# A window-attention and gated-MLP kernel on one core: the q/k/v products of two chunks as 2x2 block products, k and v parked in DRAM, attention in the background

## The chip, the core and the metric

The kernel runs on one core of a Trainium2 chip. The core has TensorE (PE in the profile; PEld are its weight loads), VectorE (DVE), ScalarE (ACT), GpSimd (POOL) and SyncE (SP), which here only issues DMA transfers. The metric is the time of one execution on the device, in microseconds (us); lower is better.

## The reference

```python
xn = layernorm(x)                      # x: 2048 x 1024, bf16
q, k, v = split(xn @ wqkv)             # 32 heads of 32
# a token at s sees the 8 tokens s, s-2, ..., s-14
attn = softmax(q . k[s - 2w] * 32**-0.5, over w = 0..7; masked below 0)
s = (sum_w attn[w] * v[s - 2w]) @ wo
h = silu(xn @ w1) * (xn @ w3)          # 1024 -> 3584
g = silu(h @ w2)                       # 3584 -> 1024
out = x + s * g
```

## The kernel before

The 2048 tokens are four chunks of 512 (`c` 0 to 3). Two chunks are a pair (`b` 0 and 1), and the MLP works on a pair. Activations lie transposed: a feature is a partition, tokens are columns. A matmul here is 128x128 by 128x512 into a bank of PSUM; there are eight banks (pool `mm`).

**Block products.** The up and down products of a pair are computed with seven block products in place of eight (Winograd's form of Strassen): rows are the two chunks, columns two halves of the output features, and the inner dimension is cut into two halves. The sums of blocks of the activations are made once a pair (`xn_sums`: `xs0` to `xs3`; `s1` to `s4` in `mlp_down`). The sums of blocks of the weights are made for pair 0 (`w_sums`, `w2_sums`), stored in DRAM (`s_dram`, `t_dram`) and read again for pair 1. In such a group ScalarE copies a bank into another (`fork`) or to SBUF (`us5`, `us2`), and VectorE adds from PSUM (`ua2`, `uh`; `dsa`, `dsb` in the down product). One up step (`up_step`) makes 256 of the 3584 features with 56 matmuls; a pair has 14. Its `tail` is put into the instruction stream of the next step (`flush`). The q, k and v products are plain: `qkv_t(c, t, ...)`, 64 matmuls for a chunk and each of q, k, v, evicted by ScalarE.

**Attention** (`attention(c)`) is VectorE work: for each of the eight positions a product of q with the shifted kT (`qk`), then a tree of sums (`qa`, `qb`, `qc`) into E; 16 DMAs on GpSimd regroup E into L (a<-E in the profile); sums `z` and the softmax; 16 DMAs write it back (E<-a); and products with the shifted vT (`pv`, `pa`), which leave the result in the place of q (`qo`). kT and vT hold one chunk and 16 tokens ahead of it, which `halo` copies on GpSimd. `wo(c)` multiplies by wo, by the gate g, and adds x.

**Order.** Every operation is recorded with its cells (`plan.op`). TensorE's order is the order of the program. The order of the other engines' instructions comes from the planner (`Plan.simulate`): it goes through all operations with fixed costs, and an engine that is free takes, of what is ready, the operation with the earliest due time (`limits`: when TensorE needs its result). On the chip each engine then works strictly in the order written, SyncE's queue of transfers included. The chunks went

```python
qkv_t(c0, ...) ; xn_sums() ; up steps 0..cut ; attention(c0)
qkv_t(c1, ...) ; up steps cut..14            ; attention(c1)
mlp_down(b)    ; wo(c0)                      # wo(c1) after the next pair's q/k/v
```

Lines in the profile are those of helpers: L299 `mm`, L308 `tt` (VectorE's additions and products), L313 `cp`, L316 `silu`, L322 `dma`, L421 the transposes of x and L428 their copies (`ln_tp`), L396, L399, L402 and L409 the layernorm on ScalarE, L448 `halo`. Tiles: `r` weights, `k` 128x512 buffers (pool `k2`), `a` attention's buffers, `xs` the sums of xn and later the gates.

Of the kernel before, what the change touches and what calls it, by code (L numbers as in the profile page):

```python
# [193 lines left out]
def kernel(  # L194
# [44 lines left out]
    t_dram = dram.tile([P, FH, 4, CH], FP16, name="t_dram")  # L239

# [8 lines left out]
    E = const.tile([P, W, CH], BF16, name="E")  # L249
# [87 lines left out]

    def gt_cell(u, i):
        return ("xs", 2 * u + i // 4, i % 4)
# [106 lines left out]
    def halo(c):  # L446
        for nm, b in (("k", kT), ("v", vT)):
            plan.op(POOL, f"halo{nm}", lambda b=b: nc.gpsimd.tensor_copy(  # L448
                out=b[:, :, 0:HALO], in_=b[:, :, CH:CH + HALO]),
                [(nm, j) for j in range(NJ)], [(nm, j, "halo") for j in range(NJ)], 0.95)  # L450

    def qkv_t(c, t, wts):
        half = c % 2
        for j in range(NJ):
            if j == 2:
                flush()
            ps = bank(f"qkv{c}_{t}_{j}")
            for hf in range(2):
                mm(ps, [qkv_w(wts[hf], k, j) for k in range(4)],
                   [lambda k=k, hf=hf: xT[:, half, hf * 4 + k, :] for k in range(4)], hf == 0,  # L460
                   [wts[hf]] + xt_cells(half, hf), last=hf == 1)
            if t == 0:
                dst, wr = (lambda j=j: qo[:, half, j, :]), qo_cells(half, [j])
            elif t == 1:
                dst, wr = (lambda j=j: kT[:, j, HALO:HALO + CH]), [("k", j)]
            else:
                dst, wr = (lambda j=j: vT[:, j, HALO:HALO + CH]), [("v", j)]
            cp(f"ev{c}_{t}_{j}", dst, ps.ap, [ps], wr)


    def attention(c):
        u = c % 2
        J4 = [range(0, 4), range(4, 8)]
        r4 = lambda s: s.ap().rearrange("p (j n) -> p j n", j=4)
        for w in range(W):
            o = HALO - DIL * w
            pr = []
            for jh in range(2):
                p_t = plan.slot("att", f"p{c}_{w}_{jh}")
                tt(f"qk{c}", mul, lambda p_t=p_t: r4(p_t), lambda jh=jh: qo[:, u, jh * 4:jh * 4 + 4, :],  # L480
                   lambda jh=jh, o=o: kT[:, jh * 4:jh * 4 + 4, o:o + CH],
                   qo_cells(u, J4[jh]) + [("k", j) for j in J4[jh]] + ([("k", j, "halo") for j in J4[jh]] if w else []),
                   [p_t], 2048, True)
                pr.append(p_t)
            p0, p1 = pr
            tt(f"qa{c}", add, lambda p0=p0: r4(p0), lambda p0=p0: r4(p0), lambda p1=p1: r4(p1), [p0, p1], [p0], 2048, True)
            tt(f"qb{c}", add, lambda p0=p0: r4(p0)[:, 0:2], lambda p0=p0: r4(p0)[:, 0:2], lambda p0=p0: r4(p0)[:, 2:4],
               [p0], [p0], 1024, True)
            tt(f"qc{c}", add, lambda w=w: E[:, w, :], lambda p0=p0: r4(p0)[:, 0], lambda p0=p0: r4(p0)[:, 1],
               [p0], [("E", w, sq, r) for sq in range(4) for r in range(NR)], 512, True)  # L490
        L = [plan.slot("att", f"L{c}_{i}") for i in range(2)]
        Lv = lambda i: L[i].ap().rearrange("p (r w n) -> p r w n", r=2, w=W)
        for r in range(NR):
            for sq in range(4):
                dma(POOL, f"L{c}", lambda r=r, sq=sq: Lv(r // 2)[sq * 32:(sq + 1) * 32, r % 2, :, :],
                    lambda r=r, sq=sq: E[r:P:NR, :, sq * P:(sq + 1) * P],
                    [("E", w, sq, r) for w in range(W)], [(L[r // 2], r % 2, sq)], 128)
# [27 lines left out]
        for r in range(NR):  # L525
            for sq in range(4):
                dma(POOL, f"E{c}", lambda r=r, sq=sq: E[r:P:NR, :, sq * P:(sq + 1) * P],
                    lambda sq=sq: pbv()[sq * 32:(sq + 1) * 32], [pb], [("E", w, sq, r) for w in range(W)], 128)
        for jh in range(2):
            js = slice(jh * 4, jh * 4 + 4)  # L530
            A = lambda js=js: qo[:, u, js, :]
            Ac = qo_cells(u, J4[jh])

            def pv(dst, wr, w, jh=jh, js=js):
                o = HALO - DIL * w
                tt(f"pv{c}", mul, dst, lambda: E[:, w, :].unsqueeze(1).to_broadcast([P, 4, CH]),
                   lambda: vT[:, js, o:o + CH],
                   [("E", w, sq, r) for sq in range(4) for r in range(NR)] + [("v", j) for j in J4[jh]]
                   + ([("v", j, "halo") for j in J4[jh]] if w else []), wr, 2048, True)

            pv(A, Ac, 0)
            B = plan.slot("att", f"B{c}")
            pv(lambda B=B: r4(B), [B], 1)
            tt(f"pa{c}", add, A, A, lambda B=B: r4(B), Ac + [B], Ac, 2048, True)
            for w0 in (2, 4, 6):
                B, C = plan.slot("att", f"B{c}"), plan.slot("att", f"C{c}")
                pv(lambda B=B: r4(B), [B], w0)
                pv(lambda C=C: r4(C), [C], w0 + 1)
                tt(f"pa{c}", add, lambda B=B: r4(B), lambda B=B: r4(B), lambda C=C: r4(C), [B, C], [B], 2048, True)
                tt(f"pa{c}", add, A, A, lambda B=B: r4(B), Ac + [B], Ac, 2048, True)  # L550
# [47 lines left out]
    def up_step(b, fb):  # L598
# [5 lines left out]
        if fb + 1 < FB and (b, fb + 1) not in tiles and fb + 1 != cut[b]:  # L604
            up_load(b, fb + 1)
# [31 lines left out]
        if b == 0 and fb + 1 < FB and fb + 1 != cut[b]:  # L637
            w_sums(fb + 1)
        for i in I:
            mm(pb[i], sl(2, i), tx[2], False, [(st, 2)] + xs_cells(2))  # L640
            tt("uh", add, hv(i, 1), pb[i].ap, lambda i=i: f32(sp5[i]), [pb[i], sp5[i]], hc(i, 1), 512, False)
            sg2.append(plan.slot("k2", "sg2"))
            silu("sg2", lambda i=i: b16(sg2[i])[:, 0:CH], lambda i=i: f32(su2[i]), [su2[i]], [sg2[i]], 0.54)
# [5 lines left out]
        def tail():  # L649
            for i in I:  # L650
                mm(pb[i], wl(1, 1, i), tx[3], False, [(wt, 1, 1)] + xs_cells(3))
                tt("um", mul, hv(i, 0), hv(i, 0), pb[i].ap, hc(i, 0) + [pb[i]], hc(i, 0), 512, False)
            for i in I:
                tt("um2", mul, hv(i, 1), hv(i, 1), lambda i=i: b16(sg2[i])[:, 0:CH], hc(i, 1) + [sg2[i]], hc(i, 1), 512, True)
# [24 lines left out]
    gts = [xsb[:, 2 * u:2 * u + 2].rearrange("p a k n -> p (a k) n") for u in range(2)]  # L679

    def mlp_down(b):
# [29 lines left out]
        gt = gts  # L711
# [27 lines left out]
        for g in G:  # L739
            prod(pa[g], g, 0, 1, rhs, False, BF16)  # L740
            silu("dg", lambda g=g: gt[0][:, g], pa[g].ap, [pa[g]], [gt_cell(0, g)], 0.48)
# [18 lines left out]
        for g in G:  # L760
            prod(pe[g], g, 0, 1, rhs, False, FP16)
            tt("dsb", add, lambda g=g: f32(su2[g]), pe[g].ap, lambda g=g: f32(su2[g]), [pe[g], su2[g]], [su2[g]], 512, False)
            silu("dg", lambda g=g: gt[0][:, NST + g], lambda g=g: f32(su2[g]), [su2[g]], [gt_cell(0, NST + g)], 0.54)
        rhs = rhs_load("t", t=T3)
        for g in G:
# [4 lines left out]
            silu("dg", lambda g=g: gt[1][:, NST + g], lambda g=g: f32(sp5[g]), [sp5[g]], [gt_cell(1, NST + g)], 0.54)  # L770
        for st in range(NST if b + 1 < NB else 0):
            ln_tp(2 * b + 3, st, xn[1])
        rhs = rhs_load("t", t=T4)
        for g in G:
            prod(pb[g], g, 1, 1, rhs, False, BF16)
            silu("dg", lambda g=g: gt[1][:, g], pb[g].ap, [pb[g]], [gt_cell(1, g)], 0.48)

    def wo(c):
        u = c % 2
        gt = gts[u]  # L780
# [17 lines left out]
        for i, (dh, st) in enumerate(grp):  # L798
            if i + 2 < len(grp):
# [6 lines left out]
            o_t = plan.slot("k2", "o_t")  # L806
            tt("o_t", mul, lambda o_t=o_t: f32(o_t), ps.ap, lambda dh=dh, st=st: gt[:, dh * NST + st],
               [ps, gt_cell(u, dh * NST + st)], [o_t], 512, False)
            x = xe[i]
            tt("x_o", add, lambda x=x: b16(x)[:, CH:D], lambda o_t=o_t: f32(o_t), lambda x=x: b16(x)[:, 0:CH],  # L810
               [o_t, (x, 0)], [(x, 1)], 512, False)
# [4 lines left out]
    cut = (11, 10)  # L816
    x0 = plan.slot("r8", "x0")
# [8 lines left out]
    for b in range(NB):  # L826
        c0, c1 = 2 * b, 2 * b + 1
        if b:
            halo(c0)
        qkv_t(c0, 0, qkv_load(0))  # L830
        if b == 0:
            x1 = plan.slot("r8", "x1")
# [4 lines left out]
        wk = qkv_load(1)  # L837
        if b == 0:
            for st in range(NST):
                ln_tp(1, st, x1)  # L840
        qkv_t(c0, 1, wk)
        qkv_t(c0, 2, qkv_load(2))
        if b == 0:
            w2_load(0)
        else:
            wo(c0 - 1)
        xn_sums()
        for fb in range(cut[b]):
            up_step(b, fb)
        attention(c0)  # L850
        halo(c1)
        wq = qkv_load(0)
        wk = qkv_load(1)
        qkv_t(c1, 0, wq)
        wv = qkv_load(2)
        qkv_t(c1, 1, wk)
        up_load(b, cut[b])
        if b == 0:
            w_sums(cut[b])
        qkv_t(c1, 2, wv)  # L860
        for fb in range(cut[b], FB):
            up_step(b, fb)
        attention(c1)
        mlp_down(b)
        wo(c0)
    wo(2 * NB - 1)
# [31 lines left out]
```

## Time and profile before

| | us |
|---|---|
| median of 3 runs (lowest, highest) | 761.17 (760.47, 761.50) |
| profiled execution | 759.42 |
| its span, first to last instruction | 757.6 |
| TensorE busy | 742.4 |
| VectorE busy | 599.4 |
| ScalarE busy | 320.1 |
| GpSimd busy | 106.8 |

DMA moved 150.56 MB, 199 GB/s on the mean. The mean granted clock of TensorE was 0.995 of full speed. Rows give the mean time of one instruction and the idle time of the engine ahead of it with what ended it; a stretch of the table of windows has, for each engine, its busy time and the number of its instructions.

### The profile page before, as it was taken

The numbers are of one execution on the slowest core, as the hardware profiler recorded it, in microseconds if no ns is written. First come the engines' busy times: TensorE is split into PE (matmuls) and PEld (weight loads), VectorE is DVE, ScalarE is ACT, GpSimd is POOL, SyncE is SP. The second block draws the span as 40 slices with busy tenths as digits, with TensorE's granted clock in tenths as the row PEclk, the third lists the DMA queues.
The fourth block names the chain that finished last, engine by engine and source line by source line (L and its number), as shares of the span: only waits on it lengthen the run. The fifth ranks groups of instructions, "written<-read, shape, count | busy, mean of one in ns | idle before, by whom it ended". The sixth has DMA issues, their size and how long they took to land.

```text
span 757.6 us, 9366 instructions
## 1 busy us (share of the span) xinstructions
PE 742.4 (98%) x3457; PEld 375.8 (50%) x3516; DVE 599.4 (79%) x830; ACT 320.1 (42%) x535; POOL 106.8 (14%) x172
## 2 busy tenths in 40 slices
PE   7999999999999999998999999999999999999997
PEld 4664444444664444453566444444466544444443
DVE  6599988899989995539937995789925987939946
ACT  5536446544335599334033144644423544311200
POOL 0000050600311006140000004400100012040000
PEclk9999999999999999999999999999999999999999
DMA  9766589776598875766762847654554457483723
GB/s 326 228 223 200 162 194 306 241 259 199 185 304 263 286 239 147 211 183 227 250 196 98 260 148 192 195 174 149 167 163 143 140 166 188 147 235 126 224 87 120
DMA packets 123117, 150.56 MB, mean 199 GB/s; under 512 B 6080, under 2 KB 97728, under 8 KB 119488
## 3 DMA queue, kind: packets, MB, share of 16 engines
q1 hardware_dynamic: 114944, 119.55, 50.3%
q0 software_dynamic: 8128, 30.42, 12.7%
q8 instruction: 27, 0.44, 0.3%
q14 instruction: 18, 0.15, 0.1%
HBM read 115.34 MB, written 26.21 MB: 187 GB/s over the span
## 4 chain that ended last, share of the span: by engine, by line
PE 84%; DVE 5%; ACT 4%; DMA 3%; issue 2%; POOL 2%; SPq 0%; DVEq 0%; ACTq 0%
PE mm L299 83%; DVE a L308 3%; DMA a<-E 2%; POOL E L322 1%; ACT k L396 1%; ACT k L399 1%; DMA E<-a 1%; DVE k L308 1%; DVE r L308 1%; DVE h_sb L308 1%; PE mm L421 1%; POOL a L322 1%; DVE small L379 0%; ACT xT L428 0%; DMA r<-in_A_x_dram 0%
## 5 line engine op out<-in xcount | busy, mean ns | idle before, releaser
L299 PEld LDWEIGHTS <-r 128*128 128x128 bf16 (+1 forms) x2336 | 263.4, 113 | 241.1 <-issue 0.7
L299 PE MATMUL mm<-xT,r 128*128 128x512 bf16 x1395 | 322.9, 379 | 2.8 <-ACT xT L428 0.5
L299 PE MATMUL mm<-xs,r 128*128 128x512 f16 x896 | 207.7, 379 | 0.0
L299 PE MATMUL mm<-r,h_sb 128*128 128x512 f16 (+1 forms) x664 | 147.8, 382 | 0.4
L308 DVE TENSOR_TENSOR a<-qo,kT 128x2048 bf16<-128x2048 bf16 x64 | 76.6, 1217 | 39.7 <-ACT kT L313 39.6
L299 PEld LDWEIGHTS <-h_sb 128*128 128x128 bf16 (+1 forms) x672 | 65.9, 98 | 79.4 <-issue 2.4
L308 DVE TENSOR_TENSOR a<-a,a 128x2048 bf16<-128x2048 bf16 (+1 forms) x72 | 87.6, 1217 | 19.4 <-DMA a<-E 19.0
L313 ACT COPY k<-mm 128x512 f32<-128x512 f32 x128 | 74.4, 586 | 55.8 <-PE mm L299 55.3
L308 DVE TENSOR_TENSOR a<-E,vT 128x2048 bf16<-128x2048 bf16 x56 | 66.0, 1215 | 0.0
L308 DVE TENSOR_TENSOR k<-mm,k 128x512 f32<-128x512 f32 x72 | 48.0, 683 | 20.0 <-PE mm L299 18.0
L316 ACT ACTIVATE k<-k 128x512 bf16<-128x512 f32 x56 | 35.0, 630 | 51.5 <-DVE k L308 51.4
L313 ACT COPY mm<-mm 128x512 f32<-128x512 f32 x64 | 36.1, 570 | 47.2 <-PE mm L299 47.0
L299 PE MATMUL mm<-r,qo 128*128 128x512 bf16 x250 | 55.4, 379 | 0.3
L316 ACT ACTIVATE h_sb<-mm 128x512 bf16<-128x512 f32 x56 | 33.4, 597 | 52.2 <-PE mm L299 52.2
L322 POOL DMA_DIRECT2D a<-E x64 | 36.9, 585 | 90.1 <-DVE E L308 80.6
L322 POOL DMA_DIRECT2D E<-a x64 | 36.7, 581 | 73.3 <-DVE a L308 69.2
L308 DVE TENSOR_TENSOR a<-a 128x1024 bf16<-128x1024 bf16 (+4 forms) x60 | 37.7, 631 | 8.6 <-DMA a<-E 7.0
L308 DVE TENSOR_TENSOR h_sb<-h_sb,mm 128x512 bf16<-128x512 bf16 x56 | 36.9, 680 | 7.6 <-PE mm L299 7.5
L313 ACT CAST qo<-mm 128x512 bf16<-128x512 f32 x32 | 18.8, 586 | 54.1 <-PE mm L299 52.9
L308 DVE TENSOR_TENSOR r<-r 128x512 f16<-128x512 bf16 (+1 forms) x84 | 39.1, 503 | 2.9 <-PE mm L299 2.9
L299 PEld LDWEIGHTS <-qo 128*128 128x128 bf16 x256 | 25.1, 98 | 30.1
L308 DVE TENSOR_TENSOR qo<-qo,a 128x2048 bf16<-128x2048 bf16 x32 | 38.9, 1214 | 0.1
(61 smaller groups left out, 435.4 us busy)
## 6 DMA issues: line engine op xcount, KB each, us to landing
r<-in_B_w_dram SPq DMA_DIRECT2D x56, 512.0 KB, 5.4
r<-in_A_wqkv_dram SPq DMA_DIRECT2D x24, 1024.0 KB, 5.4
s_dram<-r POOLq DMA_DIRECT2D x14, 1024.0 KB, 6.1
r<-t_dram SPq DMA_DIRECT2D x16, 896.0 KB, 5.8
r<-s_dram SPq DMA_DIRECT2D x14, 1024.0 KB, 5.3
r<-in_B_w_dram SPq DMA_DIRECT2D x12, 896.0 KB, 5.9
r<-in_A_wo_dram SPq DMA_DIRECT2D x8, 1024.0 KB, 7.8
t_dram<-r POOLq DMA_DIRECT2D x14, 512.0 KB, 5.7
```

The lines of the kernel that those rows point to most:

```text
L299: nc.tensor.matmul(ps.ap(), lhsT=lhs[k](), rhs=rhs[k](), start=(first and k == 0), stop=(last and k == n - 1), skip_group_check=not (first ...
L308: plan.op(DVE, name, lambda: fn(out=o(), in0=a(), in1=b()), rd, wr, occ, 0.08, late=late)
L313: plan.op(ACT, name, lambda: nc.scalar.copy(out=o(), in_=a()), rd, wr, occ, 0.11)
L316: plan.op(ACT, name, lambda: nc.scalar.activation(out=o(), in_=a(), func=ACTF.Silu), rd, wr, occ, 0.11, table="silu")
L322: plan.op(eng, name, lambda: e.dma_start(out=o(), in_=a()), rd, wr, occ, 0.0, nbytes=kb * 1024, late=late)
L396: plan.op(ACT, f"mean{c}_{st}", lambda i=i, st=st, junk=junk: nc.scalar.activation(out=b16(junk), in_=xrow(xt, st), func=ACTF.Copy, scale= ...
L399: plan.op(ACT, f"var{c}_{st}", lambda i=i, st=st, junk=junk: nc.scalar.activation(out=b16(junk), in_=xrow(xt, st), func=ACTF.Square, bias= ...
L421: nc.tensor.matmul(tp.ap()[:, k * P:(k + 1) * P], lhsT=xrow(xt, st)[:, kt * P:(kt + 1) * P], rhs=ident[:], start=(k == 0), stop=(k == KH - ...
```

## The change

- q of chunks 0 and 1 stays plain (`q_plain`), with the transposes of chunk 1 in the middle of chunk 0's q. All other q/k/v products are made for a pair at once (`qkv_pairs`), with seven block products of eight; `qkv_sums` makes the weights' block sums on VectorE each time.
- kT and vT still hold one chunk. What comes early (k and v of chunks 1 and 2; q, k and v of chunk 3) is written into parts of `h_sb` that are not yet in use, stored to DRAM from there (`put`) and fetched by `attention` (`get`). `halo` is split into k's and v's.
- Attention is recorded elsewhere: chunk 0 after all up steps, chunk 1 inside pair 1 after up step 6, followed by `wo(1)`; chunk 2 after pair 1's up steps, chunk 3 after `wo(2)`.
- E is stored as four runs of 128 tokens with the eight positions in each, so a piece of 32 partitions is one run of 2 KB; half of the pieces' DMAs are issued by SyncE.
- In the up step's tail and in `wo`, ScalarE copies the product out as bf16, and VectorE works on bf16 in SBUF alone; the two products of the tail become one of 1024 columns.
- Gates lie in other places (`gate`), and chunk 3's transposes are taken one group at a time in the last group of the down product.

```diff
-    def qkv_t(c, t, wts):
+    def q_plain(c, wts, mid=None):
...
+    def put(c, nm):
...
+        dma(SP, f"put{nm}{c}", lambda: park[nm, c][:], src, cells, [("park", nm, c)], 1024)
+    def get(c, nm):
...
+        dma(SP, f"get{nm}{c}", dst, lambda: park[nm, c][:], [("park", nm, c)], wr, 1024)
+    def qkv_sums(wts):
+        S = [plan.slot("r8", f"S{i}") for i in range(2)]
+        w = lambda kh, r: (lambda: wts[kh].ap().rearrange("p (c j) -> p c j", j=NJ)[:, :, r * 4:r * 4 + 4])
...
+        tt("qs0", add, sv(0), w(0, 1), w(1, 1), wts, c(0), 2048, True)
+        tt("qs1", sub, sv(1), sv(0), w(0, 0), c(0) + [wts[0]], c(1), 2048, True)
+        tt("qs3", sub, sv(3), w(1, 0), sv(1), c(1) + [wts[1]], c(3), 2048, True)
+        tt("qs2", sub, sv(2), w(0, 0), w(0, 1), [wts[0]], c(2), 2048, True)
+    def qkv_pairs(b, nm, wts, S, load=None):
...
+                mm(pa[i], wl(0, js[i]), bx[0, 0], True, [wts[0]] + xt_cells(0, 0))
+                mm(pe[i], sw(0, js[i]), tx[0], True, sc(0) + xs_cells(0))
+                cp("qfork", pb[i].ap, pa[i].ap, [pa[i]], [pb[i]])
+                cp("qs5", lambda i=i, s=sp5: f32(s[i]), pe[i].ap, [pe[i]], [sp5[i]])
+                mm(pa[i], wl(1, js[i]), bx[0, 1], False, [wts[1]] + xt_cells(0, 1))
+                cp("qc11", dst, pa[i].ap, [pa[i]], wr)
+                mm(pb[i], sw(1, js[i]), tx[1], False, sc(1) + xs_cells(1))
+                cp("qu2", lambda i=i, s=su2: f32(s[i]), pb[i].ap, [pb[i]], [su2[i]])
+                mm(pe[i], sw(3, js[i]), bx[1, 1], False, sc(3) + xt_cells(1, 1))
+                tt("qc12", add, dst, pe[i].ap, lambda i=i, s=su2: f32(s[i]), [pe[i], su2[i]], wr, 512, False)
+                mm(pb[i], sw(2, js[i]), tx[2], False, sc(2) + xs_cells(2))
+                tt("qc22", add, dst, pb[i].ap, lambda i=i, s=sp5: f32(s[i]), [pb[i], sp5[i]], wr, 512, False)
+                    mm(pb[i], wl(1, js[i] + 4), tx[3], False, [wts[1]] + xs_cells(3))
+                    cp("qc21", dst, pb[i].ap, [pb[i]], wr)
...
     def attention(c):
+        for nm in "qk":
+            if nm == "k" and c:
+                halo("k")
+            if (nm, c) in park:
+                get(c, nm)
...
-                dma(POOL, f"L{c}", lambda r=r, sq=sq: Lv(r // 2)[sq * 32:(sq + 1) * 32, r % 2, :, :],
-                    lambda r=r, sq=sq: E[r:P:NR, :, sq * P:(sq + 1) * P],
+                dma((POOL, SP)[sq % 2], f"L{c}", lambda r=r, sq=sq: Lv(r // 2)[sq * 32:(sq + 1) * 32, r % 2],
+                    lambda r=r, sq=sq: E[r:P:NR, sq], [("E", w, sq, r) for w in range(W)], [(L[r // 2], r % 2, sq)], 96)
...
-                tt(f"pv{c}", mul, dst, lambda: E[:, w, :].unsqueeze(1).to_broadcast([P, 4, CH]),
-                   lambda: vT[:, js, o:o + CH],
+                q4 = lambda a: a.rearrange("p j (q n) -> p j q n", n=P)
+                tt(f"pv{c}", mul, lambda: q4(dst()), lambda: E[:, :, w, :].unsqueeze(1).to_broadcast([P, 4, NST, P]),
+                   lambda: q4(vT[:, js, o:o + CH]),
...
     (tail of the up step)
-                tt("um", mul, hv(i, 0), hv(i, 0), pb[i].ap, hc(i, 0) + [pb[i]], hc(i, 0), 512, False)
+                cp("uc", lambda i=i: b16(sg2[i])[:, 0:CH], pb[i].ap, [pb[i]], [(sg2[i], 0)])
-                tt("um2", mul, hv(i, 1), hv(i, 1), lambda i=i: b16(sg2[i])[:, 0:CH], ..., 512, True)
+                tt("um", mul, lambda i=i: h_sb[:, fl[i], :], lambda i=i: h_sb[:, fl[i], :], lambda i=i: b16(sg2[i]), ..., BL, True)
...
     (wo)
-            tt("o_t", mul, lambda o_t=o_t: f32(o_t), ps.ap, lambda dh=dh, st=st: gt[:, dh * NST + st], ..., 512, False)
-            tt("x_o", add, lambda x=x: b16(x)[:, CH:D], lambda o_t=o_t: f32(o_t), lambda x=x: b16(x)[:, 0:CH], ..., 512, False)
+            cp("s_c", xv, ps.ap, [ps], [(x, 1)])
+            tt("s_g", mul, xv, xv, gv, [(x, 1)] + gc, [(x, 1)], CH, True)
+            tt("x_o", add, xv, xv, lambda x=x: b16(x)[:, 0:CH], [(x, 0), (x, 1)], [(x, 1)], CH, True)
...
     (mlp_down, last group)
-        for st in range(NST if b + 1 < NB else 0):
-            ln_tp(2 * b + 3, st, xn[1])
         rhs = rhs_load("t", t=T4)
         for g in G:
+            if b + 1 < NB:
+                ln_tp(2 * b + 3, g, xn[1])
             prod(pb[g], g, 1, 1, rhs, False, BF16)
...
     (the order)
+        qkv_pairs(b, "v", wv, sv, first)
+        for fb in range(FB):
             up_step(b, fb)
+            if b and fb == 6:
+                attention(c0 - 1)
+                wo(c0 - 1)
         attention(c0)
         mlp_down(b)
         wo(c0)
-    wo(2 * NB - 1)
+    attention(3)
+    wo(3)
```

## The prediction

> **What bounds the kernel now.** I read the busy times of the page first, then the waits of TensorE, the chain of waits that ended last, and a table of stretches around the one place where that chain leaves TensorE.
>
> ```profile
> PE 742.4 (98%) x3457; PEld 375.8 (50%) x3516; DVE 599.4 (79%) x830; ACT 320.1 (42%) x535; POOL 106.8 (14%) x172
> PE   7999999999999999998999999999999999999997
> PE mm L421 <- ACT xT L428: 3.1, 1, 3.1
> PE mm L421 <- DVE r L385: 2.6, 1, 2.6
> PE mm L299 <- ACT xT L428: 0.5, 1, 0.5
> ```
>
> TensorE is busy 98% of the span, and past the head (12.9 us) it has one long wait: 3.1 us for the transposes of x (L421). So a matmul taken away is worth its full time, provided that nobody else becomes late. The chain and the stretches show what that one wait cost:
>
> ```profile
> 269.03 0.48 ACT mm L313
> ...
> 329.96 5.63 DMA E<-a
> 343.97 0.61 DVE k L308
> 344.60 0.63 ACT xs L316
> 345.23 1.95 ACT xT L428 x4
> 347.60 13.99 PE mm L299 x57
> ```
>
> ```profile
> 341.00:347.60 6.60, 3.05 (x35) 2.16 (x34) 6.60 (x8) 4.19 (x10) 0.00 (x0) 1.00 1.00 317
> 347.60:350.00 2.40, 2.40 (x7) 0.88 (x6) 2.40 (x3) 2.05 (x5) 0.00 (x0) 0.50 1.01 372
> 350.00:352.00 2.00, 2.00 (x9) 0.75 (x7) 2.00 (x3) 0.00 (x0) 0.00 (x0) 0.75 1.04 372
> ```
>
> Attention of chunk 1 wrote its softmax back late (E<-a); VectorE, in order, held the additions of the down product (k, `dsa`) behind the products that needed E; ScalarE held the copies of the transposes (xT) behind the gates (xs) of those additions; TensorE stood still for 6.60 - 3.05 = 3.55 us, and then ran at a granted clock of 0.50 for 2.4 us and 0.75 for 2.0 us, which loses 1.2 + 0.5 = 1.7 us. The place costs 5.2 us.
>
> VectorE's price per instruction is the step from one start to the next, since ends overlap by about 0.08 us:
>
> ```profile
> 246.07 0.42 DVE L308 TENSOR_TENSOR E<-a 128x512 bf16<-128x512 bf16 x1
> 246.41 0.68 DVE L308 TENSOR_TENSOR h_sb<-h_sb,mm 128x512 bf16<-128x512 bf16 x1
> 247.01 2.35 DVE L308 TENSOR_TENSOR a<-qo,kT 128x2048 bf16<-128x2048 bf16 x2
> 249.28 0.42 DVE L308 TENSOR_TENSOR r<-r 128x512 f16<-128x512 bf16 x1
> ```
>
> 512 columns of 16 bits in SBUF: 0.34 us; 512 with an operand in PSUM: 0.60; 2048 of 16 bits: 2.27 / 2 = 1.135; by the same reading 1024 of 16 bits 0.60 (starts 256.26 and 256.86). A ScalarE eviction steps by 0.48 (first line of the chain above).
>
> **Part 1, the products.** Before, 12 products (q, k, v of four chunks) of 64 matmuls are 768. After, q of chunks 0 and 1 stays plain (128), and k, v of the first pair and q, k, v of the second are five products of 112: 688 in all. The order of TensorE's instructions has 160 fewer rows, 80 weight loads and 80 matmuls. An up step of 56 matmuls starts every 12.09 us in the chain (75.62 to 87.71), 0.2158 us each: 80 x 0.2158 = **17.3 us less**, all on the path.
>
> What the saving costs beside it, VectorE: 20 weight sums of 2048 (22.7 us by 1.135) and 40 additions out of PSUM (24.0). ScalarE: 116 evictions for 96, 9.6 us more.
>
> **Part 2, products copied out as bf16.** Up: `um` from PSUM (56 x 0.60) and `um2` (56 x 0.34) become 56 of 1024 columns (0.60): 18.8 us less. Output: 64 x 0.60 becomes 64 x 0.34: 17.0 less. ScalarE gets 56 + 32 copies, 42.2 us. So VectorE nets 46.7 - 35.8 = 10.9 us more (610 of some 736), ScalarE 51.9 more (372). Neither is a bound as a whole, and both keep room where TensorE could feel it: an up step of the first pair needs 4 x 0.60 + 4 x 0.34 + 6 x 0.60 = 7.3 us of VectorE's 12.09, and leaves 4.7 x 14 = 66 us for attention of chunk 0; ScalarE needs 12 x 0.48 = 5.8. The price is nothing while that cover holds. The last output group ends with 0.48 + 0.34 + 0.34 and their latencies instead of 2 x 0.69: the tail is the same within 0.2 us.
>
> **Part 3, the background.** Attention of chunks 0 to 3 no longer stands between q/k/v and the rest of its own chunk; it needs about 78 us of VectorE each (34.7 for QK, 9.2 softmax, 34.1 PV). By the new order chunk 0 fits in the first up steps, chunk 1 runs through the first down product, wo and the second q/k/v, chunk 2 and QK of chunk 3 in the second up steps, the rest in the second down product. In the second pair's q/k/v TensorE takes 71 us; VectorE has 34.1 (PV) + 8 x 1.135 + 24 x 0.60 = 57.6 there. At the end: 16 subtractions of the down product (16.0), softmax (12.3 with the exponential), the write-back (8.8, below) and PV with 8 additions (38.9) make 76 us from the last up step; wo of chunk 3 begins 92 us after it. It is covered by 16 us.
>
> **The stall.** Transposes of chunk 3 now stand one group at a time before the groups of the last down product, and PV of chunk 1 stands behind all four `dsa`. What made the 3.1 us wait is gone from its place: **5.2 us less**. Next in line is the gather of the logits (a<-E): the sum `z` stands before the fourth `dsa`, about 10 us after the last logits. Before, sixteen issues on GpSimd took from 293.24 to 312.1 with landing; now eight are on GpSimd (8 x 0.58 = 4.6) and eight on SyncE, in runs of 2 KB instead of 256 B. Landing is bounded by 2.4 us (x for the output, SyncE, 128 KB) and 5.3 (a<-E); I take 5.3, the same transfer: 9.9 us, just in time, with 10 us more before the fourth `dsa` holds TensorE. The write-back is 4.6 + 4.2 (E<-a) = 8.8; before the first PV of chunk 1 VectorE has 8 x 1.135 + 8 x 0.34 = 11.8 us of other work.
>
> **The queues.** SyncE issues 290 transfers for 224 (12 weight loads fewer, 14 parked ones and 64 pieces of E more). In its order the loads of the next up step stand behind the fetch of k (which waits for GpSimd's halo copy) and behind the E pieces (which wait for VectorE). The halo copy took 0.29 to 6.29 us in the trace. Up weights are issued a step ahead, 12.09 less 5.4 of landing, so 6.7 us cover it. In the head x of chunk 1 must be normalised for its first transpose at 19.8 us (12.86 and 32 matmuls); that was done at 18.3, and its loads are now ahead of all of k's weights. Left for frictions at these thin covers: 0 to 5 us, I take 1, since nearly all covers are over 3 us.
>
> **Sum.** The profiled execution took 759.42 us, its span 757.6, 1.8 outside. Span 757.6 - 17.3 - 5.2 + 1.0 = 736.1; with 1.8, 737.9. The median of the runs stood 1.75 above the profiled one: **739.7 us**.
>
> **Weights read in short runs.** No row has operands in runs of 4 elements, as the 20 weight sums read them. Bounds: 1.135 as packed rows do, or 2.2 as unpacked ones do (a step of 128x1024 f32 is about 1.13, twice that for 2048); less than 1.135 is excluded, since no row of 2048 is cheaper. I take 1.135, since the operands are 16-bit in SBUF like those rows. [...]
>
> **Rivals.**
> - *The exchange stalls come back elsewhere.* For it: VectorE waited 26.1 us for a<-E and 19.4 us for E<-a before, and SyncE now has them in front of weight loads. Against: issue time halved, longer runs, the covers above. Each such stall costs what the one of before cost, 5.2 us, in place of the 1.0 I left: two of them give 749; all eight exchanges would give 780, and five are slower than before. Chance 0.14, of which 0.01 within the bound and 0.01 slower.
> - *Weight sums unpacked.* In the second pair 12 sums cost 12 x 1.07 = 12.8 us more, against 13 us of room: 0 to 12.8 us, about 6, so 746. Chance 0.05.
> - *Slower: the E products lose the packed rate.* E now lies in four runs of 128 columns, so each PV product reads a four-dimensional, broadcast view. At 2.2 for 1.135 the 64 products add 68 us to VectorE, in an order fixed in advance. They are spread over stretches with some 7 us spare (first up steps) and 13 us (second q/k/v); half of the 68 then reaches TensorE: 739.7 + 34 = 774. It decides the sign from a third, 22 us, on. Against: the same broadcast in runs of 128 is in the softmax (a<-a,a 128x1024, f32) and takes the plain f32 step. Chance 0.07. [...]
>
> **Chances.** My forecast with up to 5 us of friction 0.74, the rivals 0.14, 0.05, 0.07. About 0.2%, 1.5 us, is what a measurement of this kernel can tell from no change. Faster 0.74 + 0.12 + 0.05 = 0.91, same 0.01, slower 0.01 + 0.07 = 0.08. The range begins where friction is nil and the tail a little shorter, 737, and reaches over two and a half exchange stalls and the whole of the unpacked sums, to 753; less than 0.1 is outside.
>
> **What would show it.** TensorE busy near 723 us (742.4 - 17.3 - 1.7), PEclk at 9 in every slice, no wait of L421 for xT around the change of pairs; VectorE near 610, ScalarE near 372; weight sums near 1.2 us each; PV rows still at 1.215. A span over 745 with TensorE waiting for ScalarE or a DMA at the exchanges would be the first rival, wrong covers in part 3; a PV row over 2 us the last. TensorE busy above 730 would mean that the matmuls are not what I counted.

## The result and the profile after

| | before | changed |
|---|---|---|
| median (lowest, highest), us | 761.34 (760.47, 761.97) | 757.30 (756.05, 757.71) |
| profiled execution, its span, us | 759.42, 757.6 | 756.05, 754.3 |

The ratio is 0.9945, with a 95% interval of 0.9928 to 0.9962: 4.0 us faster, where the prediction had 761.2 - 739.7 = 21.5 and a range that ended at 753. The matmuls are gone as forecast (PEld, the weight loads, falls from 3516 to 3436; not every matmul stands in the trace, 3457 in that of before), but one new wait of TensorE gives most of it back. First the busy times and two rows of the slices, on the page of the changed kernel:

```profile
PE 727.1 (96%) x3436; PEld 354.6 (47%) x3436; DVE 610.4 (81%) x834; ACT 384.9 (51%) x644; POOL 81.3 (11%) x108
PE   7999999999999955999999999999999999999997
PEclk8999999999999986999999999999999999999999
```

The rows of PE and of the granted clock dip in slices 15 and 16 (264 to 302 us) and, but for the head and the tail, nowhere else. The waits of TensorE name the place, and the chain that ended last says what stood in front of it (start, duration, engine, tile, line):

```profile
PE mm L301 <- DMA r<-in_B_w_dram: 17.1, 1, 17.1
PE mm L420 <- DVE r L384: 3.8, 1, 3.8
```

```profile
262.53 21.18 POOL vT L447
283.72 0.56 SPq L324
...
284.38 7.62 DMA r<-in_B_w_dram
...
292.04 7.97 PE mm L301 x30
```

L447 is the copy of v's halo on GpSimd, L324 the DMA helper, L301 `mm`. A copy of 128x128 elements takes 21.18 us; behind it SyncE issues the fetch of parked v, and behind that, in the same queue, the weights of the down product (w2, 896 KB), which have nothing to do with v. TensorE waits 17.10 us for them. The stretches show the rest of the price (columns: span, PE, PEld, DVE, ACT, POOL, PEclk, DMA share, GB/s):

```profile
262.00:275.00 13.00, 12.95 (x60) 5.78 (x59) 13.00 (x14) 13.00 (x26) 12.48 (x1) 1.00 0.17 55
275.00:279.00 4.00, 0.00 (x0) 0.00 (x0) 4.00 (x5) 3.95 (x6) 4.00 (x1) 0.84 0.01 2
279.00:292.00 13.00, 0.00 (x0) 0.00 (x0) 4.54 (x5) 0.20 (x1) 4.70 (x1) 0.50 0.53 172
292.00:294.00 2.00, 1.96 (x5) 0.69 (x5) 0.00 (x0) 0.00 (x0) 0.00 (x0) 0.50 1.09 346
294.00:296.00 2.00, 2.00 (x9) 0.82 (x8) 0.92 (x1) 0.92 (x2) 0.00 (x0) 0.81 1.09 349
```

From 275 to 279 the DMA engines are idle (0.01), though TensorE is waiting for a DMA: it had not been issued. After the wait the granted clock is 0.50 for 2 us and then 0.81 for 2 us, which loses 2 x 0.5 + 2 x 0.19 = 1.4 us. With the wait that is 18.5 us. Now the three queues at that time, as timelines of VectorE, SyncE and GpSimd of the changed kernel:

```profile
262.29 1.21 DVE L310 TENSOR_TENSOR qo<-qo,a 128x2048 bf16<-128x2048 bf16 x1
...
281.46 2.08 DVE L310 TENSOR_TENSOR h_sb<-xT,h_sb 128x1792 f16<-128x1792 f16 x2
295.08 1.09 DVE L310 TENSOR_TENSOR h_sb<-h_sb 128x1792 f16<-128x1792 bf16 x1 [11.55 <-PE mm L301]
```

```profile
259.65 1.75 SPq L324 DMA_DIRECT2D r<-in_A_x_dram  x4
283.72 0.56 SPq L324 DMA_DIRECT2D vT<-park_v  x1
284.38 0.60 SPq L324 DMA_DIRECT2D r<-in_B_w_dram  x1
```

```profile
262.52 21.18 POOL L447 COPY vT<-vT 128x128 bf16<-128x128 bf16 x1 [13.74 <-ACT k L398]
```

Between 262.29 and 283.54 VectorE runs 21 products and sums without a gap, every one with both inputs in SBUF. GpSimd's copy begins at 262.52, inside that string, and ends at 283.70, 0.16 us after it. SyncE issues nothing in between.

### The profile page after: what moved, and what is told of

Its sections match the earlier page's. It is cut to its first block, busy times and chain, and to the rows that moved or that the text cites. A ratio compares the mean times of both kernels' runs of the same rounds, so it can differ in the third digit from the quotient of the medians.

```text
span 754.3 us, 9486 instructions
## 1 busy us (share of the span) xinstructions
PE 727.1 (96%) x3436; PEld 354.6 (47%) x3436; DVE 610.4 (81%) x834; ACT 384.9 (51%) x644; POOL 81.3 (11%) x108
## 4 chain that ended last, share of the span: by engine, by line
PE 93%; POOL 3%; DMA 2%; ACT 1%; DVE 1%; issue 0%; SPq 0%; ACTq 0%
PE mm L301 92%; POOL vT L447 3%; PE mm L420 1%; DMA r<-in_B_w_dram 1%; DMA r<-in_A_x_dram 1%; DVE small L378 0%; ACT k L398 0%; ACT k L395 0%; ACT xT L427 0%; SPq L324 0%; DVE k L310 0%; ACT k L318 0%; ACT k L315 0%; DVE r L384 0%; ACT small L381 0%
## 5 line engine op out<-in xcount | busy, mean ns | idle before, releaser
L301 PEld LDWEIGHTS <-r 128*128 128x128 f16 (+1 forms) x2256 | 242.2, 108 | 244.9 <-issue 1.5
L301 PE MATMUL mm<-xs,r 128*128 128x512 f16 x1216 | 281.4, 379 | 0.0
L301 PE MATMUL mm<-xT,r 128*128 128x512 bf16 x1040 | 244.4, 380 | 0.4 <-ACT xT L427 0.4
L301 PE MATMUL mm<-r,h_sb 128*128 128x512 bf16 (+1 forms) x672 | 148.8, 381 | 17.1 <-DMA r<-in_B_w_dram 17.1
L301 PEld LDWEIGHTS <-h_sb 128*128 128x128 bf16 (+1 forms) x672 | 65.7, 98 | 95.7 <-issue 19.2
L310 DVE TENSOR_TENSOR h_sb<-mm,k 128x512 bf16<-128x512 f32 x96 | 63.2, 679 | 31.6 <-PE mm L301 31.0
L315 ACT CAST k<-mm 128x512 bf16<-128x512 f32 x88 | 51.2, 585 | 50.2 <-PE mm L301 49.1
L301 PE MATMUL mm<-r,qo 128*128 128x512 bf16 x256 | 55.7, 379 | 0.0
L310 DVE TENSOR_TENSOR h_sb<-h_sb,k 128x1024 bf16<-128x1024 bf16 x56 | 37.1, 679 | 16.1 <-ACT k L315 16.1
L310 DVE TENSOR_TENSOR r<-r 128x512 f16<-128x512 bf16 (+2 forms) x89 | 46.7, 541 | 2.5 <-DMA r<-in_B_w_dram 2.3
L447 POOL COPY vT<-vT 128x128 bf16<-128x128 bf16 x3 | 27.0, 8994 | 120.7 <-issue 55.7
L310 DVE TENSOR_TENSOR r<-r,r 128x1024 f16<-128x1024 f16 (+3 forms) x43 | 37.3, 867 | 3.0 <-PE mm L420 1.9
L301 PEld LDWEIGHTS <-qo 128*128 128x128 bf16 x256 | 25.0, 98 | 30.2
```

The source lines that it names most:

```text
L301: nc.tensor.matmul(ps.ap(), lhsT=lhs[k](), rhs=rhs[k](), start=(first and k == 0), stop=(last and k == n - 1), skip_group_check=not (first ...
L310: plan.op(DVE, name, lambda: fn(out=o(), in0=a(), in1=b()), rd, wr, occ, 0.08, late=late)
L315: plan.op(ACT, name, lambda: nc.scalar.copy(out=o(), in_=a()), rd, wr, occ, 0.11)
L447: plan.op(POOL, f"halo{nm}", lambda: nc.gpsimd.tensor_copy(out=b[:, :, 0:HALO], in_=b[:, :, CH:CH + HALO]), [(nm, j) for j in range(NJ)], ...
```

## Experiments

The theory to be tested: GpSimd's read of SBUF does not get through while VectorE works on two inputs from SBUF, so the copy lasts as long as VectorE's string beside it; SyncE's queue turns that into a late weight load. The rivals: the fetch or the load itself is slow; GpSimd is slow at whatever it does there; the block products or the new exchange cost more than forecast and hide behind this place. Medians of the kernel before beside these runs were 760.2 to 760.7.

**The halo on ScalarE** (e1).

```diff
-        plan.op(POOL, f"halo{nm}", lambda: nc.gpsimd.tensor_copy(out=b[:, :, 0:HALO], ...
+        plan.op(ACT, f"halo{nm}", lambda: nc.scalar.copy(out=b[:, :, 0:HALO], ...
```

> The changed kernel with the halo copies of k and v made by ScalarE in place of GpSimd; nothing else is edited, VectorE's order is the same. Theory A (the copy on GpSimd is held while VectorE runs products and sums with two inputs in SBUF back to back, and SyncE's queue stands behind the fetch of v that waits for the copy): the copy of v is under 1 us, the 17.1 us wait of TensorE and the 1.7 us at a lowered clock go, the span falls from 754.3 to 735.5 and the time from 757.3 to about 738.5. Theory B (the w2 weights would have been late anyway, by landing or by the number of transfers that SyncE now issues): the copy is short, but TensorE still waits for the w2 load, and the time stays above 750.

Measured: 736.96 (736.72 to 737.50), ratio to before 0.9688 (0.9674 to 0.9701); span 735.4, 18.9 us shorter than that of the changed kernel, against the 18.5 read above. (By the medians it is 20.3 us: the profiled execution of the changed kernel was its fastest, and where the others lost 0.8 to 1.7 us more no trace shows.) The wait is gone, and ScalarE makes the same copy in 0.3 us. Its page, L447 by its line, and SyncE's timeline:

```profile
PE 725.0 (99%) x3436; PEld 354.3 (48%) x3436; DVE 610.1 (83%) x834; ACT 386.0 (52%) x650; POOL 50.0 (7%) x102
```

```profile
L447 ACT COPY vT<-vT x3: 285/297/301, 281.9 to 562.3; 128x128 bf16<-128x128 bf16 x3
```

```profile
266.71 0.38 SPq L324 DMA_DIRECT2D r<-in_B_w_dram  x1
271.67 1.88 SPq L324 DMA_DIRECT2D r<-t_dram  x2
282.19 0.56 SPq L324 DMA_DIRECT2D vT<-park_v  x1
```

The w2 load is now issued at 266.71 instead of 284.38, and the fetch of v stands behind it. So the order in the queue changed too (the edit also lowers the planner's price of the copy, from 0.95 to 0.25), and this run alone does not tell a faster copy from a better order.

**The fetch of v issued by GpSimd** (e2): the slow copy stays, only SyncE does not wait for it.

```diff
-        dma(SP, f"get{nm}{c}", dst, ...
+        dma(POOL if nm == "v" else SP, f"get{nm}{c}", dst, ...
```

> The changed kernel with the fetch of v from DRAM issued by GpSimd's own queue in place of SyncE's; the halo copy stays on GpSimd, and the orders of VectorE and ScalarE are the same. Theory A: the first copy of v still takes about 21 us (15 to 22), but no weight load stands behind it, so TensorE does not wait: about 738.5 us. Theory B: TensorE still waits for w2, above 750 us. If the copy itself is short here, the lockout by VectorE is wrong.

Measured: 736.54 (736.16 to 737.40), ratio 0.9683 (0.9670 to 0.9696). GpSimd's timeline and SyncE's:

```profile
262.80 25.18 POOL L447 COPY vT<-vT 128x128 bf16<-128x128 bf16 x1 [13.74 <-ACT k L398]
288.28 0.91 POOL L324 DMA_DIRECT2D vT<-park_v  x1 [0.30 <-POOL vT L447]
```

```profile
267.27 0.38 SPq L324 DMA_DIRECT2D r<-in_B_w_dram  x1
```

The copy takes even longer, 25.18 us where I had expected 15 to 22, v comes later still, and TensorE waits for neither v nor weights. So the slow copy costs nothing by itself: the price is what SyncE had queued behind the fetch. VectorE's string ended at 287.83 in this run, and the copy at 287.98, again just behind it. The string is longer too, 25 operations in place of 21: the next four sums, which in the changed kernel had to wait for TensorE (295.08 above), now follow without a gap in 4.08 us, and the copy takes 4.00 us more.

**GpSimd writes the halo without reading** (e3; the halo's content is left out, zeros stand in its place).

```diff
-        plan.op(POOL, f"halo{nm}", lambda: nc.gpsimd.tensor_copy(out=b[:, :, 0:HALO], in_=b[:, :, CH:CH + HALO]),
+        plan.op(POOL, f"halo{nm}", lambda: nc.gpsimd.memset(b[:, :, 0:HALO], 0.0),
```

> The changed kernel with each halo copy replaced by a GpSimd memset of the same 128x128 elements: the halo's content is left out, the orders of all engines and all waits are the same. Theory A in its narrow form (it is GpSimd's reading of SBUF that VectorE's second input shuts out): the write takes under 1 us in the same place beside the same VectorE work, and the time is about 738.5 us. Theory C (any GpSimd work on SBUF starves beside VectorE, or GpSimd's times there are an artefact): the write takes many us too, TensorE waits as before, about 757 us.

Measured: 737.17 (736.53 to 737.52), ratio 0.9688 (0.9675 to 0.9702). GpSimd's timeline, and SyncE's:

```profile
262.39 0.20 POOL L447 MEMSET vT<- 128x128 bf16 x1 [13.71 <-DVE a L310]
```

```profile
262.34 0.56 SPq L324 DMA_DIRECT2D vT<-park_v  x1
266.89 0.38 SPq L324 DMA_DIRECT2D r<-in_B_w_dram  x1
```

The same engine, moment, size and target, beside the same work of VectorE: 0.20 us in place of 21.18. So neither GpSimd nor its writes are slow there; it is the read. SyncE keeps the order of the changed kernel, the fetch of v ahead of the w2 load. But the fetch begins 0.05 us before the memset: it does not wait for it, unlike my expectation that all waits are the same, since the memset reads nothing that the fetch overwrites. So the time of this run shows that the order alone does no harm. The long copy alone does none either, where no load stands behind its fetch (e2). It takes both, with the wait of the fetch between them.

**All copies of the traces.** Five traces have the halo on GpSimd: both kernels, e2, e9 and e11, six copies each. Two of the changed kernel, with VectorE's timeline beside them:

```profile
137.29 1.27 DVE L310 TENSOR_TENSOR k<-mm,k 128x512 f32<-128x512 f32 x2
425.47 1.21 DVE L310 TENSOR_TENSOR r<-r,r 128x2048 f16<-128x2048 bf16 x1
426.60 1.27 DVE L310 TENSOR_TENSOR h_sb<-mm,k 128x512 bf16<-128x512 f32 x2
```

```profile
137.54 0.29 POOL L447 COPY kT<-kT 128x128 bf16<-128x128 bf16 x1 [0.48 <-DVE a L310]
425.67 1.16 POOL L447 COPY vT<-vT 128x128 bf16<-128x128 bf16 x1 [55.72 <-issue]
```

The seven of the thirty that began beside an operation with an operand in PSUM (`mm`) took 0.29 to 0.30 us. The other 23 began beside an operation with both inputs in SBUF, took 0.64 to 25.18 us, and each ended 0.15 to 0.16 us behind the last operation of an unbroken string of such operations, in which each starts some 0.08 us before the one ahead of it ends. What broke the string was an operation with an operand in PSUM (426.60 above), a reciprocal of one input (287.76 in e2), or a gap in VectorE's work; a gap of 0.03 us was enough (208.71 to 208.74 in the kernel before), with another operation of two SBUF inputs behind it.

**The halo on ScalarE in the kernel before** (e4). The halo took up to 6.29 us there, so it might have made the stall of before too.

```diff
-            plan.op(POOL, f"halo{nm}", lambda b=b: nc.gpsimd.tensor_copy(
+            plan.op(ACT, f"halo{nm}", lambda b=b: nc.scalar.copy(
```

> The kernel before with its halo copies made by ScalarE in place of GpSimd. Its copy of k at 288.09 us took 5.01 us, with the sixteen gathers of chunk 1's logits behind it on GpSimd, which are the start of the chain to its 3.1 us wait. Theory A: that wait goes or shrinks, 5.2 us at most, so 756 us (755.5 to 760). Theory D (that wait came from the sixteen issues alone): no change, 761 us.

Measured: 760.15 (759.14 to 761.61), ratio 0.9993 (0.9984 to 1.0002): no change. Its waits keep the old stall, and GpSimd's timeline the slow write-back:

```profile
PE mm L421 <- ACT xT L428: 3.5, 2, 3.1
```

```profile
322.62 9.17 POOL L322 DMA_DIRECT2D E<-a  x16 [15.27 <-DVE a L308]
```

**The new layout of E and the shared exchange alone, in the kernel before** (e9).

```diff
-    E = const.tile([P, W, CH], BF16, name="E")
+    E = const.tile([P, NST, W, P], BF16, name="E")
...
-                dma(POOL, f"E{c}", lambda r=r, sq=sq: E[r:P:NR, :, sq * P:(sq + 1) * P],
+                dma((POOL, SP)[sq % 2], f"E{c}", lambda r=r, sq=sq: E[r:P:NR, sq],
```

> The kernel before with the new exchange of E alone: four runs of 128 tokens with eight positions each, half of the pieces issued by SyncE. If the late write-back (sixteen issues, then landing) is what made its one stall, the write-back is over 4 to 5 us sooner and most of the 5.2 us goes: 755.5 to 758. If SyncE's weight loads pay for it by standing behind the pieces, 760 or more.

Measured: 754.94 (754.09 to 755.24), ratio 0.9922 (0.9910 to 0.9934), 5.7 us less. No wait of L421 for xT is left. GpSimd issues the write-back in half the time, and VectorE's first product with E starts 6.9 us earlier than before (335.87), without a wait:

```profile
314.12 4.23 POOL L322 DMA_DIRECT2D E<-a  x8 [15.11 <-DVE a L308]
```

```profile
328.96 1.23 DVE L308 TENSOR_TENSOR qo<-E,vT 128x2048 bf16<-128x2048 bf16 x1
```

So the stall of before is worth 5.7 us, and the new layout with half the issues on another queue is enough to remove it. Which of the two does it is not separated: the write-back already begins 7.3 us earlier (314.12 for 321.39).

**The whole exchange on GpSimd again** (e6) and **chunk 3's transposes in one block again** (e8), each on e1.

```diff
-                dma((POOL, SP)[sq % 2], f"L{c}", ...
+                dma(POOL, f"L{c}", ...
-                dma((POOL, SP)[sq % 2], f"E{c}", ...
+                dma(POOL, f"E{c}", ...
```

> On e1_halo_scalar: all sixteen pieces of each exchange of E (gather and write-back) are issued by GpSimd, as before the change; the runs of 2 KB stay. The exchange takes some 4.6 us longer each way than with half of them on SyncE. If the prediction's covers hold (10 us ahead of the fourth dsa, 3 us ahead of the first PV of chunk 1, which is then 2 us short), TensorE loses 0 to 2 us: 737 to 739. If the halved issue is what removed the 5.2 us stall of the kernel before, a stall of that kind comes back: about 742.

```diff
+        for st in range(NST if b + 1 < NB else 0):
+            ln_tp(2 * b + 3, st, xn[1])
...
-            if b + 1 < NB:
-                ln_tp(2 * b + 3, g, xn[1])
```

> On e1_halo_scalar: the transposes of chunk 3 stand in one block ahead of the last group of the down product again, as before the change. They need eight banks at once behind the copies of ScalarE, which stand behind the gates of dsa. If the order of the transposes is what removed the 5.2 us stall, 2 to 5 us come back: 739 to 742. If it is attention's place and the exchange, 737 within 1 us.

Measured: 737.24 (736.64 to 737.70) and 737.99 (737.57 to 738.35), ratios 0.9689 (0.9675 to 0.9702) and 0.9700 (0.9687 to 0.9714): 0.3 and 1.0 us more than e1. In the new order either can be undone almost for nothing; I put that down to attention in the background, which is no longer due at once, but no run shows it.

**Plain products for q, k and v** (e5, on e1): the block products undone, everything else kept.

```diff
-            sq = qkv_sums(wq)
...
-            qkv_pairs(b, "q", wq, sq)
+            qkv_plain(b, "q", wq)
...
-        sv = qkv_sums(wv)
-        qkv_pairs(b, "v", wv, sv, first)
+        qkv_plain(b, "v", wv, first)
```

> On the kernel with ScalarE's halo (e1_halo_scalar): the five pair products of q, k and v are computed plain, 128 matmuls in place of 112, and the 20 weight sums and 40 additions of VectorE go with them; parking, attention's places, the exchange and the copies out stay. By the sum, 80 matmuls of 0.2158 us come back on TensorE: 17.3 us, so 737.0 + 17.3 = 754.2. Rival: the 46.7 us of VectorE that go with them had a price on the path; then less than 17.3 comes back, under 752.

Measured: 754.42 (753.78 to 754.74), ratio 0.9916 (0.9902 to 0.9929): 17.5 us more than e1.

**Products read from PSUM by VectorE again**: both places (e7, on e1), and wo alone (e12, on e1).

```diff
-                cp("uc", lambda i=i: b16(sg2[i])[:, 0:CH], pb[i].ap, [pb[i]], [(sg2[i], 0)])
+                tt("um", mul, hv(i, 0), hv(i, 0), pb[i].ap, hc(i, 0) + [pb[i]], hc(i, 0), 512, False)
...
-            cp("s_c", xv, ps.ap, [ps], [(x, 1)])
-            tt("s_g", mul, xv, xv, gv, [(x, 1)] + gc, [(x, 1)], CH, True)
+            tt("o_t", mul, lambda o_t=o_t: f32(o_t), ps.ap, gv, [ps] + gc, [o_t], 512, False)
```

> The kernel with the halo copied by ScalarE (736.96), with the copying out of products as bf16 undone in the up step's tail and in wo: VectorE again multiplies out of PSUM. By the rows VectorE gets 56 x 0.60 + 56 x 0.34 - 56 x 0.60 = 19 us more in the tails and 64 x 0.60 - 64 x 0.34 = 17 us more in wo, 646 us busy of some 737; ScalarE loses 88 copies of 0.585, 51 us. Theory: VectorE's room (4.7 us of each up step, 13 us in the second q/k/v) takes it, the attention only comes later: 736.5 to 739. Rival: the copies are what makes room for attention in the background, and TensorE waits for VectorE: 19 us less room in the first up steps push chunk 1's attention on by as much, up to 755.

> The kernel with the halo copied by ScalarE (736.96), with only the copying out in wo undone; both undone took 751.43. VectorE has 17 us more there, and the banks of wo wait for VectorE instead of ScalarE. Theory A (the two waits of 4.7 us with both undone belong to wo, whose banks and buffers come free late while VectorE works on products of attention): most of the 14.5 us is here, 745 to 752. Rival B (they come from the 19 us in the up steps, which push attention back): 737 to 741.

Measured: 751.43 (750.57 to 752.67), ratio 0.9882 (0.9868 to 0.9896), and 747.95 (746.42 to 748.51), ratio 0.9830 (0.9816 to 0.9845): 14.5 and 11.0 us more than e1. My expectation for e7 (736.5 to 739) was wrong, and wo makes most of it. The waits of TensorE and two stretches of e7, then the waits of e12:

```profile
PE mm L301 <- ACT mm L315: 4.7, 1, 4.7
PE mm L301 <- DVE qo L310: 4.7, 1, 4.7
```

```profile
523.00:544.00 21.00, 15.98 (x72) 7.13 (x73) 20.84 (x26) 2.57 (x5) 0.00 (x0) 1.00 0.90 293
690.00:730.00 40.00, 35.46 (x163) 15.97 (x163) 39.77 (x43) 5.43 (x9) 0.00 (x0) 0.98 0.38 120
```

```profile
PE mm L301 <- DVE k L310: 7.8, 2, 7.4
```

In the mean VectorE has room in e7 (644.7 us of 750.4), but from 523 to 544 us, in and behind wo of chunk 1 (its matmuls end at 532.9), it is busy for 20.84 of 21.00, and from 690 to the end of attention of chunk 3 for 39.77 of 40.00. VectorE works on wo's outputs in its order, between attention's products. In e12 TensorE then waits 7.4 us for a bank that VectorE has not yet read. In e7 it waits for ScalarE's copy from bank to bank; ahead of that, in ScalarE's order, stands a copy into a `k2` buffer, and the buffer comes free only when an output of wo has left (by the chain, at 543.07). The edit gives each output of wo one such buffer more, as before the change, so the price is not that of reading PSUM alone. The second wait of e7 is for the result of attention of chunk 3, at 730.28. The waits, and the lower clock behind them (0.50 to 0.70 in e7; in e12 the 12 matmuls from 543.32 on take 5.28 us, where 16 take 3.62 otherwise), come to 9.9 + some 4 of e7's 14.5 us, and to 7.8 + some 3 of e12's 11.0. ScalarE is not short of time there: in e7 it waits 18.1 us on end for VectorE. With the copies, ScalarE frees wo's banks itself, in e1 one every 1.7 us.

**Only the up step's tail from PSUM, halo on GpSimd** (e11): the changed kernel with `uc` undone as in e7, and wo as changed.

> The changed kernel (halo on GpSimd, 757.3) with only the copying out in the up step's tail undone: two products of 512 again, the first out of PSUM. VectorE has 19 us more work in the tails and 56 more operations that read PSUM. Theory A (GpSimd's read of SBUF waits until VectorE comes to an operation with an operand in PSUM, and the bf16 copies took such operations out of VectorE's order): v's halo beside the last up step takes less than 7 us, the wait of TensorE for the down product's weights shrinks from 17.1 to under 5 us, and the time is 738 to 748, by what the 19 us cost. Rival B (the string of products and weight sums has no room for GpSimd either way): the halo takes over 15 us again, and the time is 755 or more.

Measured: 737.93 (737.50 to 738.29), ratio 0.9703 (0.9690 to 0.9716). The halo stays on GpSimd, VectorE has 16 us more work, and the kernel is 19.4 us faster than the changed one. The timelines of VectorE, GpSimd and SyncE:

```profile
288.03 1.21 DVE L310 TENSOR_TENSOR qo<-qo,a 128x2048 bf16<-128x2048 bf16 x1
289.16 0.17 DVE L404 RECIPROCAL small<-small 128x4 f32<-128x4 f32 x1
```

```profile
288.26 1.13 POOL L447 COPY vT<-vT 128x128 bf16<-128x128 bf16 x1 [46.79 <-DVE a L310]
```

```profile
266.98 0.38 SPq L324 DMA_DIRECT2D r<-in_B_w_dram  x1
271.95 13.96 SPq L324 DMA_DIRECT2D r<-t_dram  x4
289.42 0.56 SPq L324 DMA_DIRECT2D vT<-park_v  x1
```

The time lies at the lower edge of my theory's 738 to 748, but the way is another: the products with v end some 26 us later, so the copy falls beside an operation that a reciprocal of one input follows, and is through in 1.13 us; and the planner puts the fetch behind the weight loads. That operations which read PSUM would have let the copy through at the old place is not shown by this run; that copies beside such operations are through in 0.29 to 0.30 us elsewhere, the traces show. It was luck that the copy and the string missed each other here, at 1.13 us for 21.18: the 26 us by which the products with v came later were enough.

**The halo on VectorE** (e10), in line with the string.

```diff
-        plan.op(POOL, f"halo{nm}", lambda: nc.gpsimd.tensor_copy(out=b[:, :, 0:HALO], ...
+        plan.op(DVE, f"halo{nm}", lambda: nc.vector.tensor_copy(out=b[:, :, 0:HALO], ...
```

> The changed kernel with the halo copied by VectorE instead of GpSimd, where it stands in line with the operations that hold GpSimd off. [...] Theory (GpSimd's reads are kept out by VectorE's): as with ScalarE, 736.5 to 737.5. Rival (a halo in line on VectorE comes too late for the fetch, since VectorE works through a string of older products first): the fetch waits some us, the weight load behind it too, 737.5 to 742.

Measured: 737.26 (736.59 to 737.41), ratio 0.9691 (0.9678 to 0.9704); a copy of 128x128 elements takes 0.19 us. It is as good as ScalarE (736.96). The versions that mend the failed place alone and compute the whole result are e1, e2 and e10, at 736.5 to 737.3.

## Why the prediction was wrong, and where it was right

**The step that failed** is in "The queues": "The halo copy took 0.29 to 6.29 us in the trace", and "so 6.7 us cover it". Both terms were mis-sized. The duration was read as the copy's own; the copy alone takes 0.29 to 0.30 us (seven on GpSimd, and ScalarE's in e1), and the rest is VectorE's string beside it, which the change made longer: 21.18 us. In the sum it stood under the 1.0 us for frictions, where 18.5 was due. And the cover was worked out for the weights of an up step, while the load behind the fetch is the second one of the down product. In e1 it is issued at 266.71 and lands 4.6 us later, at 271.3. In the changed kernel TensorE runs out at 274.94; e1 stands 0.29 us earlier at this place (its matmuls of the group begin at 266.94 for 267.23), so it needs the load at 274.65, and the cover is 3.3 us. Against e1's place, shifted by 0.29 to 267.0, the load was issued 284.38 - 267.0 = 17.4 us late and landed in 7.6 instead of 4.6: 17.4 + 3.0 - 3.3 = 17.1, the wait that was measured.

The trace of before held the hint: six copies of one size took from 0.29 to 6.29 us, a spread that no price of the copy explains; both of 0.3 us began beside an operation with an operand in PSUM. The runs show what made it: in the same place, beside the same VectorE operations with two inputs in SBUF, GpSimd took 21.18 us for the copy, which reads SBUF (the changed kernel), and 0.20 for the write alone (e3). The copy began at 262.52, inside an operation of VectorE's that began at 262.29, and was kept out not for that one instruction but for 21 in a row, to 283.54, as if each next one of VectorE's came ahead of it unless a gap was left. By what means VectorE keeps the read out, no run shows.

Of the rivals, none named this. The range's upper end, 753, was made of exchange stalls and unpacked weight sums, and neither came; what came was the mechanism of "SyncE now has them in front of weight loads", with the halo's fetch in place of the exchange and 18.5 us in place of 5.2.

**The other terms.**
- *The products*, 17.3 us: e5 gives 754.42 - 736.96 = 17.5. TensorE's busy time was forecast near 723 us; it is 725.0 in e1 and 727.1 in the changed kernel.
- *The stall of before*, 5.2 us: e9 gives 760.68 - 754.94 = 5.7. The sum put its end down to the new places of the transposes and of PV; e9 shows that the new exchange, layout and shared issue together, ends it without them, and e8 that in the new order the transposes' places are worth 1.0.
- *The sum*: span 736.1 was forecast, and e1, without the failed step, has 735.4. The friction of 1.0 was 0.3 by the sum's own terms, and 1.0 if the measured 17.5 and 5.7 are put in their place. Adding the 1.75 between median and profiled execution was of no use: e1's profiled execution took 737.19, its median is 736.96.
- *Part 2 at nothing*: right in the sum, but the room that made it so was judged by means. Undone it costs 14.5 us (e7), since VectorE is full for 20 and 40 us on end where wo needs it. The 16 us of cover at the end of the kernel hung on the bf16 copies too: with both undone TensorE waits there (730.28), with wo alone undone it does not.
- *VectorE* 610 us: 610.4. Small slips of the working moved nothing: its own steps give 19.0 and 16.6 for the 18.8 and 17.0 of part 2, and 336 matmuls by 0.2158 are 72.5 us, not the 71 of part 3. *ScalarE* 372: 384.9, mainly because a copy lasts 0.585 us where the sum used the step of 0.48.
- *The weight sums and PV*: 1.217 and 1.216 us, as the rows of 2048 before (1.214 to 1.219), so these two rivals did not come. By form, in the changed kernel:

```profile
L310 DVE TENSOR_TENSOR r<-r,r 128x2048 f16<-128x2048 bf16 x10 | 12.2, 1217 | 2.5 <-PE mm L420 1.9 <-PE mm L301 0.6
L310 DVE TENSOR_TENSOR qo<-E,vT 128x2048 bf16<-128x2048 bf16 x8 | 9.7, 1216 | 11.8 <-DMA E<-a 11.6
```

The second row also shows that the exchange still keeps VectorE waiting, 11.6 us for E<-a; none of it reaches TensorE, which waits for nothing of the exchange.

## What to carry over

Where a duration varies twentyfold between equal instructions, as the halo copy's did (0.29 to 6.29 us), find what runs beside them before the number goes into a sum, and ask whether the change makes the neighbour longer. In a queue that is worked in order, as SyncE's was (it issued nothing from 261.40 to 283.72 us), follow each waiting transfer to the load right behind it, by name, and take the cover from that load; here the transfer that waited for GpSimd's slow copy was better issued from GpSimd's own queue (e2: 736.54 us for 757.30). And room for work in the background is read from the stretches where it must run, not from the share of the span.

## What the runs showed of the hardware

- A GpSimd copy of 128x128 elements that reads SBUF took 0.29 to 0.30 us beside a VectorE operation with an operand in PSUM (7 of 30). Beside unbroken strings of VectorE operations with two inputs in SBUF (the other 23) it ended 0.15 to 0.16 us behind the string, at most after 21.18 us (changed kernel) and 25.18 us (e2); a gap of 0.03 us in VectorE's work let it through. A memset of the same size in the place of the 21.18 us took 0.20 us (e3).
- Longer runs did not clearly make the exchange's pieces land earlier: 64 KB between SBUF and SBUF landed in 5.3 us (a<-E) and 4.2 us (E<-a) before, in runs of 256 B, and in 6.2 and 5.1 us after, in runs of 2 KB. I had counted on 5.3 and 4.2. With runs of 2 KB the medians differ from run to run as much: 4.9 (e5) and 6.3 us (the changed kernel) for a<-E, 3.3 (e5) and 5.3 us (e1) for E<-a. The DMA issues of the changed kernel (KB each, median us to landing):

```profile
a<-E SPq DMA_DIRECT2D x32, 64.0 KB, 6.2
a<-E POOLq DMA_DIRECT2D x32, 64.0 KB, 6.3
E<-a SPq DMA_DIRECT2D x32, 64.0 KB, 5.1
E<-a POOLq DMA_DIRECT2D x32, 64.0 KB, 5.2
```

Pieces issued by SyncE and by GpSimd land within 0.1 us of each other here, but 0.9 us apart in e5 (5.8 and 4.9 us for a<-E). With all of them on GpSimd (e6) the two were 5.4 and 4.6 us.
